# Products of zeros put among TensorE's instructions in a sparse-attention and mixture-of-experts kernel

## Chip, cores and metric

One core of a Trainium2 chip runs the whole kernel. The metric is the device time of one execution in microseconds (us), the median of several runs. The engines are named as the profile names them: PE is TensorE (PEld its weight loads), DVE is VectorE, ACT is ScalarE, POOL is GpSimd, SP issues most DMAs.

## What is computed

Two stages follow each other. The first is attention with 8 batches, 8 heads, 576 positions and 64 columns a head; half of the heads look back over 31 positions, the other half at every 32nd position. The second takes the 4608 rows of 512 columns that come out, sends each to two of eight experts and adds their weighted outputs.

```python
scores = np.where(masks, scale * q @ k.T, -1e9)          # local or strided mask by head
attn   = exp(scores - max) / (sum + 1e-9)
x      = (attn @ v).transpose(0, 2, 1, 3).reshape(4608, 512)
noisy  = x @ w_gate + log1p(exp(x @ w_noise)) * noise     # 8 experts
top2, top2_w = two largest of noisy, softmax of them
for e in range(8):                                        # w1: 512 x 1024, w2: 1024 x 512
    out[rows of e] += top2_w * (relu(x[rows of e] @ w1[e]) @ w2[e])
```

## The kernel before, in words

The program is recorded as a list of pieces. A piece has an engine, an assumed duration, what it reads and writes, and a rank; `issue_all` takes them one by one, always the one that can start earliest by the planner's own clock (`now` for each engine, `free` for each of the eight PSUM banks A to H), and emits its instructions. So the order on every engine is set by the planner's assumed durations, while the chip runs that order at its own pace. `left_a` counts PE's pieces of the attention that are still to come.

The attention goes in 32 units, one for two heads of a batch, local and strided by turns. For each unit PE transposes keys and queries (`tr` in `prep`, lines 510 and 514), adds masks and multiplies queries by keys (555, 562), transposes the exponentials `ex` that ACT writes at line 593, block by block (`tr` in `item`, 603), multiplies them by the values (622, 627) and transposes the finished block `xo` (693, 689). DVE and ACT read every bank in between: maxima (589), exponentials, copies (288, 289, 291), the scaled output `xo` (643). After each batch `route` computes the gate, the two experts of each row, and a place in the expert's list. SP brings q, k, v and writes zeros to the output; POOL scatters the list's entries.

The experts' work is cut into 32 jobs, four for each expert, of 256 or 384 rows, or of 256 with a tail of 64. The early jobs are planned between the pieces of the attention. A job has a first layer (`layer1`: for each of 8 blocks of 128 hidden columns 12 products with the rows as moving columns, line 1057) and a second layer (`layer2`: products of 512 columns, line 1107). Both split each number into a high and a low part, so three products stand for one. In the first layer of a job with a tail, branches on the expert's length (`half_used`) choose the width; in the second layer `half_block` computes the tail, or, where the tail is not used, writes one product of zeros of 512 columns (line 1116) so that the bank is defined.

At the start `issue_all` emits 20 products of zeros (line 337, `warm` is a bf16 view of a tile of zeros) into bank H. They are the only such products ahead of the change apart from line 1116.

Of the kernel before, what the change touches and what calls it, by code (L numbers as in the profile page):

```python
# [22 lines left out]
def kernel(  # L23
# [12 lines left out]
    nc = tc.nc  # L36
# [59 lines left out]
    warm = zeros.bitcast(BF16)  # L96
# [199 lines left out]
    def issue_all(expert_banks, t_start):  # L296
        now = dict(t_start)
        free = {t: 0.0 for t in BANKS}
        held, filler = [0], [False]
        marks, paced = {"ACT": [], "DVE": []}, [0.0]  # L300
        left_a = sum(1 for o in pieces if not o.expert and o.eng == "PE")
        owed = 0.0
        wire = 0.0
        for o in pieces:
            o.need = len(set(o.deps) | set(o.order))
            o.next = []
        for o in pieces:
            for x in set(o.deps) | set(o.order):
                x.next.append(o)
        for o in pieces:  # L310
            for s in o.psums:
                s.left = len(s.users)
        ready = [o for o in pieces if o.need == 0]

        def at(o, e):
            t = max(now[e], o.t0)
            for x in o.deps:
                t = max(t, x.end + (o.far if x.lat else HOP[x.e].get(e, 150)))
            for x in o.order:
                t = max(t, x.start)  # L320
            if o.lat and e == "SP":

                t = max(t, wire - (1500 if o.bulk else 5000))
            if o.psums:
                n = len(o.psums)
                if o.expert and left_a and held[0] >= expert_banks:
                    return None
                if len(free) < n or not o.expert and e == "PE" and filler[0] and (
                        len(BANKS) - len(free) - held[0] + n - 1 >= ATT_BANKS):
                    return None  # L330
                t = max(t, sorted(free.values())[n - 1] + 220)
            return t


        pw = psum.tile([128, 512], F32, name="bankH")
        for i in range(NWARM):
            nc.tensor.matmul(pw[:, :256], warm[:, :128], warm, start=True, stop=True)
        now["PE"] += 214.0 * NWARM
        done = 0
        while ready:  # L340
            best = None
            per = {}
            filler[0] = any(o.expert and o.psum for o in ready)
            for o in ready:
                for e in (("ACT", "DVE") if o.eng == "ANY" else (o.eng,)):
                    t = at(o, e)
                    if t is not None:
                        per.setdefault(e, []).append((t, o.rank, o))
            for e, c in per.items():
                m = min(x[0] for x in c)  # L350
                x = min((y for y in c if y[0] <= m + 120), key=lambda y: (y[1], y[0]))
                if e == "PE" and left_a and owed > 0:

                    x = min((y for y in c if y[2].expert and y[0] <= now["PE"] + 120), key=lambda y: (y[1], y[0]), default=x)
                if x[2].eng == "ANY":
                    other = [y for y in per.get("DVE" if e == "ACT" else "ACT", []) if y[2] is x[2]]
                    if other and other[0][0] + (40 if e == "ACT" else 0) < x[0]:
                        continue
                if best is None or x[0] < best[0]:
                    best = (x[0], e, x[2])  # L360
            t, e, o = best
            o.e, o.start = e, t
            for s in o.alloc:
                s.t = s.ring.fixed[s.ring.hist.index(s) % s.ring.k] if s.ring.fixed else s.ring.make()
            for s in o.psums:
                s.tag = min(free, key=lambda x: free[x])
                del free[s.tag]
                s.t = psum.tile([128, 512], F32, name="bank" + s.tag)
                s.x = o.expert
                held[0] += o.expert  # L370
            last = o.fn(o)
            if e in marks and getattr(last, "ins", None) is not None:
                marks[e].append((o, last))
            if e == "POOL" and o.lat:


                for engine in ("DVE", "ACT"):

                    behind = [x for x in marks[engine][-40:] if paced[0] < x[0].end <= t - 200]
                    if behind:  # L380
                        x = max(behind, key=lambda x: x[0].end)
                        for y in last if isinstance(last, list) else [last]:
                            tc.add_manual_dep(y.ins, x[1].ins.name, mybir.DependencyInfo(
                                mybir.DependencyClass.Sync, mybir.DependencyReason.DATA), reason="in its time")
                        break
                paced[0] = t
            d = o.dur if not isinstance(o.dur, dict) else o.dur[e]
            now[e] = t + d
            o.end = t + d
            if o.lat:  # L390
                wire = max(wire, t + d + 650) + o.lat * o.wires / RATE
                o.end = wire + 1500
            for s in o.touch:
                if s.ring is None:
                    s.left -= 1
                    s.last = max(getattr(s, "last", 0), o.end)
                    if s.left == 0:
                        free[s.tag] = s.last
                        if s.x:
                            held[0] -= 1  # L400
            if e == "PE" and not o.expert:
                left_a -= 1
            if e == "PE":
                owed = max(-1500.0, owed - d) if o.expert else min(3000.0, owed + PACE * d) if filler[0] else 0.0
            ready.remove(o)
            done += 1
            for x in o.next:
                x.need -= 1
                if x.need == 0:
                    ready.append(x)  # L410
        assert done == len(pieces), (done, len(pieces))
# [495 lines left out]
    def experts(zero):  # L907
# [129 lines left out]
        def half_used(e):  # L1037
            if e not in counts:
                counts[e] = nc.values_load(over[:1, E + 1 + e:E + 2 + e], engines=[mybir.EngineType.PE], min_val=0,
                                           max_val=NTOK)  # L1040
            return counts[e]

        def layer1(n, f, rank):
            e, (start, nb, tail, hb) = jobs[n]
            width = nb * 128 + tail
# [4 lines left out]
            ps = Slot()  # L1050
# [3 lines left out]
            def products(which, width):  # L1054
                for m in which:
                    d, a, c = todo[m]
                    nc.tensor.matmul(ps.t[:, :width], a.t[:, 128 * d:128 * d + 128], c.t[:, d, :width], start=(m == 0),  # L1057
                                     stop=(m == len(todo) - 1))

            def mm(o):  # L1060
                last = len(todo) - 1
                if not tail:
                    return products(range(last + 1), width)

                products([0], width)
                with tc.If(half_used(e) > tail // 2) as used:
                    products(range(1, last), width)
                with used.Else():
                    with tc.If(half_used(e) > 0) as some:
                        products(range(1, last), width - tail // 2)  # L1070
                    with some.Else():
                        products(range(1, last), width - tail)
                products([last], width)
            Piece("PE", 12 * 0.4555 * width + 30, mm, rank, read=[xh, xl, whi, wlo], psum=ps, expert=True,
                  after=lengths_known if tail else [])
            Piece("ACT", act(width) + 30, lambda o: nc.scalar.activation(hh.t[:, :width], ps.t[:, :width], AF.Relu), rank,
# [119 lines left out]
    for u in range(NU):  # L1196
# [10 lines left out]
        if u % (2 * NP) == 2 * NP - 1:  # L1207
            route(units[u][0], rank + 9, init, gates)
    experts(zero)
    issue_all(4, {"PE": 1000.0, "ACT": 2000.0, "DVE": 4500.0, "POOL": 14000.0, "SP": 600.0})  # L1210

    actx.close()
# [5 lines left out]
    with tc.If(longest > CAP):  # L1218
        with ExitStack() as octx:
# [4 lines left out]
            for e in range(E):  # L1224
                left = nc.values_load(over[:1, e:e + 1], engines=ENG, min_val=0, max_val=NTOK - CAP)
                with tc.If(left > 0):
                    nc.sync.dma_start(w1t, dram(w1, e * DM * FF, [[FF, 128], [128 * FF, ND], [1, FF]]))
                    nc.sync.dma_start(w2t, dram(w2, e * DM * FF, [[DM, 128], [128 * DM, NF], [1, DM]]))
                    with tc.For_i(0, left, 128) as it:
# [20 lines left out]
                        for f in range(NF):  # L1250
                            ph = psO.tile([128, 128], F32, name="oph", bufs=2)
                            for d in range(ND):
                                nc.tensor.matmul(ph, w1t[:, d, 128 * f:128 * f + 128], xt[:, d, :],
                                                 start=(d == 0), stop=(d == ND - 1))
# [4 lines left out]
                        o = ow.tile([128, DM], F32, name="oo")  # L1259
# [30 lines left out]
```

## Time and profile before

| what | us |
|---|---|
| median of 3 runs | 1081.55 |
| lowest, highest | 1073.44, 1081.84 |
| the profiled execution, its own time | 1080.12 |
| its span, first to last instruction | 1078.3 |
| mean granted clock of TensorE over the span | 0.981 of full speed |

The times of rows and stages are those of the one profiled execution; its span is 1.8 us shorter than its time. A busy PE in the profile is a PE with an instruction under way, not one at its peak rate.

### The profile page before, as it was taken

To read this page: it belongs to the slowest core of one execution; us is meant where nothing else is said; L and a number is where in the kernel's file an instruction comes from. 1 tells how busy PE (TensorE), PEld (TensorE's weight loads), DVE (VectorE), ACT (ScalarE), POOL (GpSimd) and SP (SyncE) were. 2 spreads that over 40 slices of the span, in tenths; PEclk is the share of its full clock that TensorE was granted. 3 is DMA by queue.
4 is the path that set the end of the run, shared out by engine and by line. 5 is a ranking of instruction groups with operands and counts; after the bars stand their busy time and mean duration, and the time that the engine had idled before them with its cause. 6 is when DMAs were issued, how large, how long until landed. Compare 5 with 4: busy or idle time off the path is not lost.

```text
span 1078.3 us, 23248 instructions
## 1 busy us (share of the span) xinstructions
PE 1049.8 (97%) x8637; PEld 936.9 (87%) x8637; DVE 559.2 (52%) x1536; ACT 477.1 (44%) x1203; POOL 543.6 (50%) x661
## 2 busy tenths in 40 slices
PE   8989999999999999999999999999999999999995
PEld 7767788988888999999998989898989898899994
DVE  6878887865863145427562455245524542363330
ACT  6878787866762234225342234223422432252220
POOL 1044354516153576647575556464636564766321
PEclk8998899999999999999999999999999999999998
DMA  8998989979871235426563245225522552352221
GB/s 178 238 227 185 216 200 259 210 209 214 245 188 42 37 65 139 111 45 171 117 173 57 51 105 144 45 51 121 130 45 56 121 128 43 63 152 53 42 36 23
DMA packets 168429, 133.01 MB, mean 123 GB/s; under 512 B 51864, under 2 KB 136344, under 8 KB 168296
## 3 DMA queue, kind: packets, MB, share of 16 engines
q1 hardware_dynamic: 145160, 92.31, 33.5%
q0 software_dynamic: 23136, 38.94, 19.7%
q8 instruction: 82, 1.34, 0.5%
q14 instruction: 51, 0.42, 0.1%
HBM read 92.85 MB, written 39.39 MB: 123 GB/s over the span
## 4 chain that ended last, share of the span: by engine, by line
PE 90%; ACT 3%; DVE 2%; issue 2%; DMA 1%; POOL 0%; SPq 0%; POOLq 0%; ACTq 0%; DVEq 0%
PE bankB L1107 6%; PE bankE L1107 5%; PE bankA L1107 5%; PE bankC L1107 5%; PE bankH L1057 5%; PE bankF L1107 5%; PE bankC L1057 5%; PE bankG L1057 5%; PE bankE L1057 5%; PE bankF L1057 5%; PE bankB L1057 5%; PE bankD L1057 5%; PE bankA L1057 5%; PE bankG L1107 4%; PE bankH L1107 3%; PE bankD L1107 3%
## 5 line engine op out<-in xcount | busy, mean ns | idle before, releaser
L980 POOL DMA_INDIRECT xg<-x_dram,gxx x248 | 257.0, 1036 | 157.0 <-DVE xr L1019 77.3
L1143 POOL DMA_INDIRECT out_dram<-res,tabt x80 | 136.1, 1701 | 100.8 <-ACT res L289 58.2
L829 POOL DMA_INDIRECT tab<-ent,addr x96 | 93.1, 970 | 61.2 <-issue 19.0
L1019 DVE STREAM_TRANSPOSE xr<-xg 128x512 f32<-128x512 f32 (+1 forms) x66 | 68.2, 1033 | 44.1 <-DMA xg<-x_dram,gxx 42.7
L1028 DVE TENSOR_TENSOR xlo<-xr,xhi 128x512 fp32r<-128x512 f32 (+1 forms) x66 | 43.6, 660 | 37.1 <-ACT xhi L1026 36.1
L1026 ACT CAST xhi<-xr 128x512 fp32r<-128x512 f32 (+1 forms) x66 | 38.9, 589 | 50.0 <-DVE xr L1019 50.0
L900 DVE TENSOR_TENSOR w1lo<-wraw,w1hi 128x512 fp32r<-128x512 f32 x80 | 54.5, 686 | 3.7 <-ACT w1hi L899 0.8
L900 DVE TENSOR_TENSOR w2lo<-wraw,w2hi 128x512 fp32r<-128x512 f32 x80 | 51.6, 683 | 0.9 <-ACT w2hi L899 0.6
L899 ACT CAST w1hi<-wraw 128x512 fp32r<-128x512 f32 x80 | 48.8, 616 | 3.2 <-DMA wraw<-in_moe_w_dram 2.9
L989 POOL TENSOR_SCALAR gix<-tabt 128x2 int32<-128x2 int32 (+1 forms) x32 | 8.1, 253 | 81.3 <-DMA tabt<-tab 79.9
L899 ACT CAST w2hi<-wraw 128x512 fp32r<-128x512 f32 x80 | 46.8, 617 | 2.1 <-DMA wraw<-in_moe_w_dram 1.3
L1057 PE MATMUL bankH<-xhi,w1hi 128*128 128x256 f32 (+3 forms) x132 | 39.9, 303 | 0.0
L1057 PE MATMUL bankC<-xhi,w1hi 128*128 128x256 f32 (+3 forms) x132 | 39.9, 302 | 0.0
L1057 PE MATMUL bankG<-xhi,w1hi 128*128 128x256 f32 (+3 forms) x132 | 39.8, 302 | 0.0
L1057 PE MATMUL bankH<-xhi,w1lo 128*128 128x256 f32 (+3 forms) x132 | 39.4, 299 | 0.0
L1057 PE MATMUL bankC<-xhi,w1lo 128*128 128x256 f32 (+3 forms) x132 | 39.4, 299 | 0.0
L1057 PE MATMUL bankC<-xlo,w1hi 128*128 128x256 f32 (+3 forms) x132 | 39.3, 298 | 0.0
L1057 PE MATMUL bankH<-xlo,w1hi 128*128 128x256 f32 (+3 forms) x132 | 39.3, 298 | 0.0
L817 POOL COPY ent<-wt 96x12 f32<-96x12 f32 x8 | 2.0, 249 | 73.8 <-DVE wt L811 73.7
L1057 PE MATMUL bankG<-xhi,w1lo 128*128 128x256 f32 (+3 forms) x132 | 39.1, 297 | 0.0
L1057 PE MATMUL bankG<-xlo,w1hi 128*128 128x256 f32 (+3 forms) x132 | 39.0, 296 | 0.0
L1107 PE MATMUL bankB<-w2hi,hhi 128*128 128x512 f32 x96 | 38.9, 405 | 0.0
(678 smaller groups left out, 3543.5 us busy)
## 6 DMA issues: line engine op xcount, KB each, us to landing
wraw<-in_moe_w_dram SPq DMA_DIRECT2D x160, 256.0 KB
out_dram<-zeros SPq DMA_DIRECT2D x12, 768.0 KB
ks<-in_k_dram SPq DMA_DIRECT2D x15, 320.0 KB
qs<-in_q_dram SPq DMA_DIRECT2D x15, 320.0 KB
vraw<-in_v_dram SPq DMA_DIRECT2D x30, 160.0 KB
raw<-in_k_dram SPq DMA_DIRECT2D x16, 288.0 KB
v_l<-in_v_dram SPq DMA_DIRECT2D x16, 288.0 KB
raw<-in_q_dram SPq DMA_DIRECT2D x16, 288.0 KB
```

Of the source, the lines that this page charges most:

```text
L817: nc.gpsimd.tensor_copy(s["ent"].t[:, :, :, 1].bitcast(F32), s["wt"].t)
L829: st = nc.gpsimd.indirect_dma_start(out=tab, out_offset=bass.IndirectOffsetOnAxis(ap=s["addr"].t[:, t, kk:kk + 1], axis=0), in_=s["ent"].t ...
L899: Piece("ACT", 620, lambda o: nc.scalar.copy(hi.t, raw.t), rank, read=[raw], alloc=[hi], expert=True)
L900: Piece("DVE", 715, lambda o: nc.vector.tensor_tensor(lo.t, raw.t, hi.t.bitcast(F32), ALU.subtract), rank, read=[raw, hi], alloc=[lo], exp ...
L980: dma(lambda o, g=g: nc.gpsimd.indirect_dma_start(out=xg.t[:, g, :], out_offset=None, in_=x_dram[:4 * known, :], in_offset=bass.IndirectOf ...
L989: nc.gpsimd.tensor_scalar(gi.t[:, :nb], tb.t[:, :nb, 0], known - 1, None, op0=ALU.min)
L1019: Piece("DVE", 8.8 * rows, lambda o, xg=xg, xr=xr, ng=ng, rows=rows: nc.vector.transpose(xr.t.rearrange("p (c x) -> p c x", c=ND)[:, :, :r ...
L1026: Piece("ACT", 620 * rows // 128, lambda o, view=view, cols=cols: nc.scalar.copy(xh.t[:, :, cols], view()), rank, read=[xr], expert=True, ...
L1028: Piece("DVE", 725 * rows // 128, lambda o, view=view, cols=cols: nc.vector.tensor_tensor(xl.t[:, :, cols], view(), xh.t[:, :, cols].bitca ...
L1057: nc.tensor.matmul(ps.t[:, :width], a.t[:, 128 * d:128 * d + 128], c.t[:, d, :width], start=(m == 0), stop=(m == len(todo) - 1))
L1107: nc.tensor.matmul(ps.t, HT[n, f][p[0]].t[:, cols], W2[n][f][p[1]].t, start=(m == 0), stop=(m == len(todo) - 1))
L1143: st = nc.gpsimd.indirect_dma_start(out=out[:known, :], out_offset=bass.IndirectOffsetOnAxis(ap=places(), axis=0), in_=y.t[:rows, :], in_o ...
```

## The change

Two kinds of products of zeros are added, each one weight load of zeros and one product of 256 columns in bf16.

The first stands in `issue_all`: as long as there are pieces of the attention to come, a PE piece with one bank that starts later by the planner's clock than PE and its bank allow is preceded by products into that same bank, one for each 150 ns of the planned gap after the first 150. The piece's own first product starts its accumulation anew. The planner's clock is not advanced for them.

The second stands in `layer1`: a job of 256 columns without a tail gets one product of zeros into its bank ahead of its first product.

```diff
             for s in o.psums:
                 s.tag = min(free, key=lambda x: free[x])
+                bank_free = free[s.tag]
                 del free[s.tag]
...
+            if e == "PE" and left_a and len(o.psums) == 1:
+                room = t - max(now["PE"], bank_free + 220)
+                for i in range(int((room - 150) // 150)):
+                    nc.tensor.matmul(o.psums[0].t[:, :256], warm[:, :128], warm, start=True, stop=True)
             last = o.fn(o)
...
             def mm(o):
                 last = len(todo) - 1
                 if not tail:
+                    if f == 0 and width == 256:
+                        nc.tensor.matmul(ps.t[:, :256], warm[:, :128], warm, start=True, stop=True)
                     return products(range(last + 1), width)
```

In the changed program 137 products of the first kind stand in 32 groups of 1 to 14, all ahead of the first product of line 1057, and 16 of the second kind. Apart from them the order of all five engines is the same. In the changed program the old lines from 369 on are 5 higher, those behind line 1062 are 7 higher.

PE's order in the attention, at about 123 us of the trace of before (`ks`, `ex` and `xo` are operands of transposes), before:

```order
L514 MATMUL bankF<-ident,qs 128x72 x4
L514 MATMUL bankC<-ident,ks 128x72 x4
L603 MATMUL bankG<-ident,ex 72x128 x4
L693 MATMUL bankH<-ident,xo_147 128x128 x4
L603 MATMUL bankE<-ident,ex 72x128 x4
```

The same place in the changed program, from the last of six pairs ahead of bank G on:

```order
L375 LDWEIGHTS zeros
L375 MATMUL bankG<-zeros 128x256
L608 MATMUL bankG<-ident,ex 72x128 x4
L375 LDWEIGHTS zeros
L375 MATMUL bankH<-zeros 128x256
L375 LDWEIGHTS zeros
L375 MATMUL bankH<-zeros 128x256
L698 MATMUL bankH<-ident,xo_147 128x128 x4
L608 MATMUL bankE<-ident,ex 72x128 x4
```

Six pairs stand now ahead of the transposes into bank G and two ahead of those into bank H; nothing else moved.

PE's order where a job of 256 columns follows the second layer of the job before it, before:

```order
L1107 MATMUL bankC<-w2hi,hhi 128x512
L1107 MATMUL bankC<-w2lo,hhi 128x512
L1107 MATMUL bankC<-w2hi,hlo 128x512
L1057 MATMUL bankA<-xhi,w1hi 128x256
L1057 MATMUL bankA<-xlo,w1hi 128x256
```

The same place in the changed program:

```order
L1114 MATMUL bankC<-w2hi,hhi 128x512
L1114 MATMUL bankC<-w2lo,hhi 128x512
L1114 MATMUL bankC<-w2hi,hlo 128x512
L1069 LDWEIGHTS zeros
L1069 MATMUL bankA<-zeros 128x256
L1062 MATMUL bankA<-xhi,w1hi 128x256
L1062 MATMUL bankA<-xlo,w1hi 128x256
```

One pair stands now between the two layers, into the bank of the job's first block.

## Rows read from the trace of the kernel before

**Rows 1.** The page: busy us, share of the span and instructions of each engine

```profile
PE 1049.8 (97%) x8637; PEld 936.9 (87%) x8637; DVE 559.2 (52%) x1536; ACT 477.1 (44%) x1203; POOL 543.6 (50%) x661
```

**Rows 2.** Busy time by stage; columns as in the first line

```profile
core 0: us, PE busy (x) PEld busy (x) DVE busy (x) ACT busy (x) POOL busy (x), PEclk, DMA share, GB/s
...
13.80:24.04 10.24, 10.24 (x116) 8.78 (x116) 6.60 (x20) 6.35 (x19) 0.00 (x0) 0.50 0.77 162
24.04:85.48 61.44, 54.12 (x1011) 44.08 (x1007) 49.77 (x214) 51.10 (x173) 13.40 (x29) 1.00 0.93 229
85.48:95.72 10.24, 9.85 (x102) 8.38 (x104) 7.96 (x23) 7.98 (x23) 6.01 (x12) 0.50 1.01 197
95.72:116.20 20.48, 18.19 (x292) 14.23 (x290) 17.59 (x80) 17.40 (x58) 6.45 (x13) 1.00 0.86 185
116.20:126.44 10.24, 10.24 (x116) 8.88 (x114) 6.75 (x27) 6.82 (x22) 4.56 (x8) 0.50 0.82 200
126.44:143.76 17.32, 16.43 (x321) 13.47 (x317) 15.10 (x50) 13.60 (x43) 11.88 (x23) 1.00 1.00 224
...
352.71:1053.99 701.28, 701.28 (x4206) 641.20 (x4204) 304.75 (x556) 225.89 (x457) 402.54 (x396) 1.00 0.40 88
```

**Rows 3.** Chain of waits by line: 116.20 to 126.44 us, then 24.04 to 85.48 us

```profile
by line: PE bankD L562 10.7%; PE bankB L622 10.4%; PE bankG L603 8.3%; PE bankH L693 8.3%; PE bankE L603 8.3%; PE bankE L510 6.6%; PE bankC L510 5.7%; PE bankF L514 4.7%; PE bankG L514 4.7%; PE bankC L514 4.7%; PE bankD L555 4.2%; PE bankB 
...
by line: ACT ex L593 8.8%; DMA raw<-in_k_dram 5.9%; issue 3.8%; PE bankE L603 3.6%; PE bankA L622 3.1%; ACT kT_s L288 2.9%; DVE mi L766 2.7%; ACT ex L595 2.7%; DVE xT L291 2.5%; DVE xo L643 2.4%; PE bankG L739 2.3%; PE bankF L603 2.2%; ACT 
```

**Rows 4.** Chain of waits in order of time: start us, us on the chain, what

```profile
1.12 4.45 PE bankH L337 x20
...
28.57 1.54 ACT ex L593 x8
...
75.86 3.63 DMA raw<-in_k_dram
103.02 6.53 DMA v_l<-in_v_dram
```

**Rows 5.** Timeline of PE: start us, us, instruction, [idle us before <- what ended it]

```profile
10.54 0.94 PE L603 MATMUL bankA<-ident,ex 128*72 128x128 f32 x4 [0.49 <-ACT ex L593]
...
28.84 0.93 PE L603 MATMUL bankH<-ident,ex 128*72 128x128 f32 x4
...
34.70 1.01 PE L603 MATMUL bankD<-ident,ex 128*96 128x128 f32 x4 [0.34 <-ACT ex L593]
...
56.99 0.63 PE L693 MATMUL bankC<-ident,xo 128*128 128x128 f32 x4 [1.53 <-ACT ex L593]
57.46 0.60 PE L603 MATMUL bankG<-ident,ex 128*72 128x128 f32 x4
57.89 0.27 PE L689 MATMUL bankH<-ident,xo 128*128 128x128 f32 x1
59.08 0.69 PE L622 MATMUL bankA<-v_s,aT 72*64 72x65 f32 x16 [0.91 <-DVE aT L291]
...
81.13 0.69 PE L622 MATMUL bankE<-v_l,aT 96*64 96x65 f32 x16
...
85.83 1.11 PE L693 MATMUL bankB<-ident,xo 128*128 128x128 f32 x4 [0.90 <-DVE xo L643]
...
97.50 1.01 PE L603 MATMUL bankD<-ident,ex 128*96 128x128 f32 x4 [0.62 <-ACT ex L593]
...
113.06 1.00 PE L603 MATMUL bankC<-ident,ex 128*96 128x128 f32 x4 [0.91 <-ACT ex L593]
```

**Rows 6.** Line 1057 in two jobs: stretch, us, PE busy, PEld busy, PEclk, DMA

```profile
843.25:854.56 11.31, 11.31 (x96) 11.26 (x95) 1.00 0.70 160
...
943.20:954.27 11.07, 11.07 (x96) 11.01 (x96) 1.00 0.65 164
```

**Rows 7.** Timeline ahead of these jobs: a weight load, a product of zeros

```profile
843.03 0.19 PEld L1057 LDWEIGHTS bankB<-xhi,w1hi 128*128 128x128 f32 x1
...
943.16 0.39 PE L1116 MATMUL bankC<-zeros 128*128 128x512 bf16 x1
```

## The prediction

> **What bounds the kernel now.** I read the page first, then the busy table by stage, then the chain of waits in the early stages, the timeline of PE there, and last the first-layer jobs one by one.
>
> The page says PE: 97% busy over the span [rows 1]. The table by stage says where that is not the whole story [rows 2]. From 352.71 us to 1053.99 us PE has no idle time at all, so there every added column of PE work is added to the end, and every column saved is taken off it. Before that lies the attention, where PE, DVE, ACT and the DMA queues are all at 75 to 100% and none is the bound alone. Whatever time the attention saves reaches the end, because the experts' PE work behind it is a fixed amount without gaps; what it loses does too.
>
> [...] Ahead of the falls PE had idled: 0.49 us at 10.54, and 0.91 us at 113.06; the 0.90 us that ended at 85.83 began ahead of the fall at 85.48 [rows 5]. But idling alone does not tell a fall: 1.53 and 0.91 us at 56.99 and 59.08 [rows 5] are the longest of all, and the clock stayed up.
>
> **The change, part by part.** It takes nothing away and moves nothing; each engine's order is what it was, with 153 weight loads and products of zeros put into PE's.
>
> *Price of one.* The 20 products of the same form at the start took 4.45 us [rows 4], 0.22 each, at a time from which no clock is recorded; 256-column products of the first layer take 11.31 / 96 = 0.118 us at full clock [rows 6]. I take 0.11 us at full clock (half of 0.22) and 0.22 at half.
>
> *137 in the attention.* Matching the order with the timeline, 58 of them (groups of 6, 6, 14, 7, 7, 8 and 10) stand just ahead of the seven instructions that have an idle time [rows 5]. 14 at 0.11 make 1.54 us against 1.53 idle, 10 make 1.10 against 0.91, 7 make 0.77 against 0.91 and 0.90, 8 make 0.88 against 0.62, 6 make 0.66 against 0.49 and 0.34. Where they are longer than the idle time, the transposes of `ex` behind them are mostly paced by ACT, which writes it block by block, and catch up. Cost about nothing.
>
> The other 79 stand where PE had no idle time in the trace: the planner's clock believed in a gap that the chip did not have. All of them on the path would be 79 x 0.11 = 8.7 us. Of these, 21 (ahead of 11.38, 28.84, 63.82, 70.00 and 113.97) stand ahead of transposes such as those at 28.84, which at full clock follow each other every (0.93 - 0.27) / 3 = 0.22 us where those at 56.99 take (0.63 - 0.3) / 3 = 0.11 [rows 5]; the 0.22 is ACT's pace (eight activations in 1.54 us on the chain at 28.57, [rows 4]), so a late start is made up. 26 stand in the three stretches at half clock (10, 8 and 8); if the clock holds, PE's work there halves and they fall into the slack. 32 are left, 3.5 us of delay on PE, the largest group of them 11 ahead of the values at 81.13 [rows 5], 1.2 us. What is late next is an evacuation by DVE or ACT, and some of the delay is found back in the next wait. I take +2.5 us; the bounds are 0 and +8.7. Each first product also takes over the wait for its bank that the real instruction had; all of PE's queue stands behind it, as it did before, and the planner puts it 220 ns after the bank's planned release, so I give that no price.
>
> *The three stretches at full clock.* Upper bound: PE is the whole path and its time halves, 3 x 10.24 / 2 = 15.4 us. Lower bound if all three go: DVE's work in them is 6.60 + 7.96 + 6.75 = 21.3 us, and in the stretch 24.04 to 85.48 DVE keeps 49.77 / 61.44 = 0.81 of the time [rows 2], so 21.3 / 0.81 = 26.3 us would do for what took 30.7: 4.4 us saved. DMA is a cover of the same kind: it is at 0.93 in the long stretch [rows 2], and the chain already waits for loads at 75.86 and 103.02 [rows 4]. The three times of the kernel lie 8.4 us apart, about what three falls more or less would make. I take -7.0, nearer to the DVE bound than to the PE bound. If no fall goes, it is 0.
>
> Whether the clock holds: the zeros of the warm-up were followed by full clock, so such products count as work, and ahead of each of the three falls stand groups of them (10 at 10.5 to 11.4, 11 at 81.1 and 7 at 85.8, 15 from 111 to 114). [...]
>
> *16 ahead of the first-layer jobs of 256 columns.* PE has no gap there, so each is paid: 0.11 us, or up to 0.19 if the next weight load (0.19 us, [rows 7]) is exposed; 16 make +1.8 to +3.0. But the 14 jobs from 352 us on come in two sorts. Eleven take 11.31 us like the one at 843.25; three take 11.07 like the one at 943.20 [rows 6]. What differs is what stands ahead: in those three the product of zeros for an unused half block, at 943.16 [rows 7]. With that product the job ends at 954.27, so the two together take 11.11 us, less than the 11.31 of the job alone: the products run at about 0.113 instead of 0.118 us, and keep that for the whole job. A lead of 256 columns instead of 512 should do the same for 11.00. Then eleven jobs save 0.31 (0.20 if it costs as much as the long one), 2.2 to 3.4; the three pay 0.11 for nothing, and so do the two jobs amid the attention: -0.55. I take -2.2. Bounds -2.9 and +3.0.
>
> **Sum**, against the profiled execution (span 1078.3, time 1080.12, within 1.5 us of the median 1081.55): 1080.1 - 7.0 + 2.5 - 2.2 = 1073.4 us.
>
> **Rivals.**
> - *The clock holds, and PE was the path.* The chain rows for it [rows 3], DVE's share and the DMA against it. -15 instead of -7: 1080.1 - 15 + 2.5 - 2.2 = 1065.4. [...]
> - *The lead does not set the pace.* For it: it has half the columns of the product seen to do so, and the jobs after wide real products have the slow pace too. +2.4 in place of -2.2: 1078.0.
> - *One or two falls stay or come elsewhere*, since the zeros shift the idle times rather than remove them: 2.3 to 4.7 us given back, 1075.7 to 1078.1.
> - *Slower: the clock falls as before.* Then the 79 lie on a path that is PE's in those stretches, 26 of them at 0.22: 53 x 0.11 + 26 x 0.22 = 11.5, of which some 8 reach the end, and the leads cost 3.0: 1080.1 + 8 + 3 = 1091. It decides if the granted clock is still 0.50 for some 30 us of the attention. For it: 56.99 and 59.08 show that idle time does not tell a fall; against it, where the groups stand.
>
> **How the numbers follow.** Forecast as summed 0.42, PE as the path 0.17, no pace from the lead 0.17, falls left 0.14, slower 0.10. About 1% (10.8 us) is what a measurement of this kernel can tell from no change: faster means under 1070.7, slower over 1092.4. The first rival is faster, and so is the part of the forecast where the stretches give 10 or more (0.12 of the 0.42); the slower rival lies just at the other bound, and I put 0.07 of it beyond. Faster 0.29, same 0.64, slower 0.07. The range 1063 to 1084 takes in the first three rivals and stops short of the slower one.
>
> **What would show it.** The table by stage: granted clock 1.00 from 24 us (or 7 us) to the tail, and the first first-layer product some 5 us ahead of 143.76. The jobs of 256 columns at 10.9 us behind their lead instead of 11.31, all alike. The transposes at the seven idle places start when they did, less what came earlier. Wrong: a stretch at 0.50 within the attention; jobs still at 11.31; idle times of DVE and ACT that now end on PE's products of zeros, or loads on the chain in the place of PE's rows.

## The result and the profile after

| | us |
|---|---|
| before, median of 16 runs | 1081.83 (1073.44 to 1086.1) |
| changed, median of 16 runs | 1070.15 (1068.19 to 1073.68) |
| ratio | 0.9896, 95% interval 0.9882 to 0.9911 |
| profiled execution of the changed kernel: time, span | 1068.83, 1067.1 |
| its granted clock over the span | 0.996 |

The changed kernel is faster by 1.04%, 11.7 us between the medians. The forecast was 1073.4 with a range of 1063 to 1084; a second measurement of the same kernel, further below, gave a ratio of 0.9923.

The page's first lines of the changed kernel, busy time and the span in 40 slices, answer to [rows 1]:

```profile
PE 1045.7 (98%) x8790; PEld 932.9 (87%) x8790; DVE 558.4 (52%) x1536; ACT 475.8 (45%) x1203; POOL 543.5 (51%) x661
...
PEclk9999999999999999999999999999999999999998
```

PE holds 153 products more and is busy 4.1 us less (1049.8 before), as it would be if work that ran at half clock now runs at full. No slice but the last has a clock under 9. The busy table by stage, cut where [rows 2] was cut and then at the first first-layer product, has the same columns as there:

```profile
13.80:24.04 10.24, 10.20 (x206) 8.50 (x205) 8.71 (x32) 8.31 (x23) 0.00 (x0) 1.00 0.98 207
24.04:85.48 61.44, 59.59 (x1030) 49.64 (x1020) 51.08 (x214) 51.80 (x177) 15.40 (x33) 1.00 1.00 227
85.48:95.72 10.24, 10.13 (x193) 8.69 (x194) 9.24 (x28) 9.40 (x32) 7.66 (x15) 1.00 1.12 220
95.72:116.20 20.48, 18.93 (x313) 15.62 (x312) 17.33 (x88) 16.89 (x54) 5.07 (x12) 1.00 0.96 223
116.20:126.44 10.24, 10.18 (x204) 8.99 (x203) 9.55 (x31) 9.16 (x31) 8.07 (x16) 1.00 1.01 228
126.44:135.10 8.66, 8.19 (x145) 6.61 (x141) 7.33 (x24) 6.99 (x23) 6.29 (x11) 1.00 1.07 239
135.10:344.06 208.96, 207.37 (x2356) 180.88 (x2355) 142.38 (x525) 138.37 (x388) 91.48 (x149) 1.00 0.80 193
344.06:1042.61 698.55, 698.55 (x4220) 636.34 (x4219) 304.13 (x556) 225.21 (x457) 401.77 (x395) 1.00 0.42 89
```

All three falls, the stretches that [rows 2] has at 0.50 (PE alone on the chain in the row for 116.20, [rows 3]), are at 1.00, and in the same 10.24 us DVE does 8.71, 9.24 and 9.55 us of work where it did 6.60, 7.96 and 6.75. The first product of the first layer starts at 135.10 us where it started at 143.76: 8.66 us gained in the attention, 8.65 of which are still there at the first job that PE does without a gap (344.06 against 352.71). PE's last instruction ends 11.38 us earlier than before, so the experts give another 2.7. DMA, at 0.92 of the time up to the first first-layer product before, is now at 1.00.

The timeline of PE at four places, the columns as in [rows 5]; line 375 is the new product in the attention, line 1069 the one ahead of a job:

```profile
52.57 1.69 PE L375 MATMUL bankC<-zeros 128*128 128x256 bf16 x14
54.17 0.66 PE L698 MATMUL bankC<-ident,xo 128*128 128x128 f32 x4
...
77.39 1.36 PE L375 MATMUL bankE<-zeros 128*128 128x256 bf16 x11
78.68 0.69 PE L627 MATMUL bankE<-v_l,aT 96*64 96x65 f32 x16
...
105.99 1.25 PE L375 MATMUL bankC<-zeros 128*128 128x256 bf16 x10
108.02 1.00 PE L608 MATMUL bankC<-ident,ex 128*96 128x128 f32 x4 [0.78 <-ACT ex L598]
...
832.49 0.28 PE L1069 MATMUL bankB<-zeros 128*128 128x256 bf16 x1
832.53 0.36 PE L1062 MATMUL bankB<-xhi,w1hi 128*128 128x256 f32 x1
832.73 0.28 PE L1062 MATMUL bankB<-xlo,w1hi 128*128 128x256 f32 x1
```

The 14 products fill what was 1.53 us of idle time and nothing is idle ahead of line 698. The ten at 105.99 leave 0.78 us idle, since ACT is still the later one there. The busy time of line 1062 (1057 before) in the jobs:

```profile
832.46:843.51 11.05, 11.05 (x98) 11.02 (x98) 8.80 (x16) 6.25 (x14) 5.95 (x7) 1.00 0.71 161
932.05:943.06 11.01, 11.01 (x98) 11.00 (x97) 8.80 (x16) 6.92 (x15) 7.09 (x6) 1.00 0.68 163
```

The first is the job that stood in [rows 6] with 11.31 us: from the start of its lead at 832.49 to its end at 843.51 it takes 11.02, so 0.29 less with the lead than without. The second was one of the three quick ones.

### The profile page after: what moved, and what is told of

It is laid out like the page before. It is cut to its first block, busy times and chain, and to the rows that moved or that the text cites. A ratio compares the mean times of both kernels' runs of the same rounds, so it can differ in the third digit from the quotient of the medians.

```text
span 1067.1 us, 23536 instructions
## 1 busy us (share of the span) xinstructions
PE 1045.7 (98%) x8790; PEld 932.9 (87%) x8790; DVE 558.4 (52%) x1536; ACT 475.8 (45%) x1203; POOL 543.5 (51%) x661
## 4 chain that ended last, share of the span: by engine, by line
PE 89%; ACT 3%; DVE 2%; issue 2%; DMA 2%; POOL 0%; POOLq 0%; DVEq 0%; ACTq 0%
PE bankB L1114 6%; PE bankE L1114 5%; PE bankA L1114 5%; PE bankC L1114 5%; PE bankF L1114 5%; PE bankC L1062 5%; PE bankG L1062 5%; PE bankE L1062 5%; PE bankH L1062 5%; PE bankF L1062 5%; PE bankA L1062 5%; PE bankD L1062 5%; PE bankB L1062 4%; PE bankG L1114 4%; PE bankH L1114 3%; PE bankD L1114 3%
## 5 line engine op out<-in xcount | busy, mean ns | idle before, releaser
L1150 POOL DMA_INDIRECT out_dram<-res,tabt x80 | 133.7, 1671 | 100.6 <-ACT res L289 51.5
```

What stands on the lines that cost most here:

```text
L1150: st = nc.gpsimd.indirect_dma_start(out=out[:known, :], out_offset=bass.IndirectOffsetOnAxis(ap=places(), axis=0), in_=y.t[:rows, :], in_o ...
```

## The experiments

The theory to be tested: the attention's 8.7 us come from the clock, which no longer falls, and the zeros there cost little; the 2.7 us of the experts come from the leads. The rivals: the zeros do cost what the forecast had, and the clock gives more; or one part does it all.

Ten runs were made, the last with the changed kernel again, each beside runs of the kernel before on the same chip. The medians of before differ by over 1 us between them (1081.75 to 1083.15), so ratios are compared.

**Each part alone.** The first kernel leaves the leads out, the second the products in the attention:

```diff
 first kernel, in layer1
-                    if f == 0 and width == 256:
-                        nc.tensor.matmul(ps.t[:, :256], warm[:, :128], warm, start=True, stop=True)
 second kernel, in issue_all
-            if e == "PE" and left_a and len(o.psums) == 1:
-                room = t - max(now["PE"], bank_free + 220)
-                for i in range(int((room - 150) // 150)):
-                    nc.tensor.matmul(o.psums[0].t[:, :256], warm[:, :128], warm, start=True, stop=True)
```

> The 137 products of zeros in the planned gaps of the attention, without the 16 ahead of the first-layer jobs. My theory (the attention gains some 8.7 us because the granted clock stays at full, and the 16 leads gain 2.7 us by the pace of eleven jobs): granted clock 1.00 through the attention, eleven jobs of 256 columns at 11.31 us again, about 1072.9 us. Rival (the leads' gain in one profile is an accident of the order of jobs and gives nothing in the time): 1070.2 us.

> The 16 leads alone, no products of zeros in the attention. My theory: stretches at granted clock 0.50 in the attention as before, all jobs of 256 columns at 10.9 us behind their lead, 1081.8 - 2.7 = 1079.1 us. Rival (leads give nothing): 1081.8 us. Second rival (the attention's gain was made in the experts, by the leads): near 1073.

Measured: the attention's part alone 1073.73 us, ratio 0.9911 (0.9876 to 0.9945); the leads alone 1080.76 us, ratio 0.9971 (0.9948 to 0.9993), before 1083.15. Both parts gain, some 9.6 and 3.1 us by the ratios, and together they make about the whole. The leads' gain agrees with 2.7 us, but with its interval of 0.8 to 5.6 us the time alone would not settle it. The jobs do: in the profile without leads eleven jobs of 256 columns take 11.31 us and three 11.08, as before, and in the profile of the leads alone all fourteen take 10.98 or 10.99 from their first real product on.

The busy table of the kernel with leads alone, cut at the stretches that its clock spent at half:

```profile
9.27:19.51 10.24, 9.51 (x99) 7.43 (x99) 5.76 (x14) 6.61 (x19) 0.00 (x0) 0.50 1.08 223
57.05:63.88 6.83, 6.26 (x72) 5.08 (x72) 3.88 (x13) 4.76 (x14) 5.14 (x10) 0.50 1.04 225
87.77:91.18 3.41, 3.36 (x18) 2.85 (x19) 3.01 (x12) 2.85 (x10) 2.60 (x5) 0.50 1.25 206
98.01:101.42 3.41, 3.41 (x25) 2.88 (x26) 2.42 (x5) 3.23 (x13) 1.68 (x3) 0.50 0.85 173
118.49:128.73 10.24, 10.24 (x117) 8.77 (x121) 6.24 (x26) 6.31 (x22) 4.32 (x7) 0.50 0.85 219
```

The order in the attention is that of before to the last instruction, and the clock falls five times instead of three, at other places: at 57 us too, where it stayed in the trace of before. So a place is no safe sign of a fall, and the three falls that the forecast looked at were three of several possible ones.

**Price of half clock.** Every run has its mean granted clock, and the stretches read from these profiles stand at 0.50 or at 1.00; so the time at half clock is put at 2 x (1 - clock) x span (41 us in the profiled execution of before, where the stretches at 0.50 add up to 40.55). Over the 40 runs of before that stood beside the first eight experiments, the time rises by 0.30 us for each us at half clock (standard error 0.05); their mean is 45 us. In the profiled execution of before 9.83 us at half clock lie in the tail behind the last product, from 1068.52 on. The slope is a correlation between executions: a delay elsewhere could both bring a fall and add time of its own, and these runs do not separate the two. The 30.7 us of the profiled execution are then worth 9.2 us, where the forecast had 7.0 between bounds of 4.4 and 15.4.

**Where the zeros stand.** Of the 32 groups the next kernels keep some, by a counter over the groups in the planner's loop:

```diff
+                zeros_now = int((room - 150) // 150)
+                if zeros_now > 0:
+                    group[0] += 1
-                for i in range(int((room - 150) // 150)):
+                for i in range(zeros_now if group[0] in KEPT else 0):
```

> Of the 137 only the 58 that stand where the trace of before shows PE idle, in seven groups, no leads. If zeros that lie on no idle time cost what my forecast had for them (2.5 us), and the clock holds with 58: 1072.9 - 2.5 = 1070.4 us. If the other 79 are free: 1072.9 with full clock. If the 79 are needed to hold the clock: one or two stretches at 0.50, 3 us each, 1076 to 1079.

> The other part of the 137: only the 79 products of zeros that stand where the trace of before shows no idle time, none in the seven idle times, no leads. If what holds the clock is that the idle times are filled: stretches at 0.50 as before and the price of 79 products on top, 1083 us or more. If it is the amount of plain products, wherever they stand: clock at 1.00 and about 1073 to 1075 us. Seen beside the run with 58 it also tells the price of a product outside the idle times: 21 more than there are 2.3 us of PE.

> Only the seven groups (43 products) that stand in the 4 us ahead of the three falls of the trace of before, no leads. If a fall is a matter of its place alone, the clock holds and the time is that of the run with 58, 1073.0 us, or a little less. If other idle times lead to falls as soon as these are gone (the clock's falls lie at other times in other executions), one or two stretches at 0.50, at 0.34 us for each us at half clock (the slope over the runs of before) 3 to 7 us more: 1076 to 1080.

Measured: the 58 in the idle times 1072.99 us, ratio 0.9905 (0.9873 to 0.9937); the other 79 alone 1078.53, ratio 0.9978 (0.9955 to 1.0002); the 43 ahead of the three falls 1075.96, ratio 0.9949 (0.9932 to 0.9965). The granted clock goes with it: the median over each kernel's runs is 0.9935, 0.9855 and 0.9895, before 0.979 and 0.978. So the 58 that fill idle time hold the clock about as well as all 137 (0.9945), the 79 hold it a little, against both sides of what was expected, and the 43 hold it less often than the 58, as expected if falls lie at other places in other executions.

**Twice as many.**

```diff
-                for i in range(int((room - 150) // 150)):
+                for i in range(2 * int((room - 150) // 150)):
```

> Twice as many products of zeros in each planned gap (274), no leads; 137 more at 0.108 us are 14.8 us more of PE. If PE's time beside the attention is free (DVE, ACT and DMA set the pace), within 2 us of the run with 137 alone, so under 1075. If a product of zeros there costs as my forecast had it (a third to a half of the exposed ones), about 1079. If PE is the path: 1087.

Measured: 1079.57 us, ratio 0.9973 (0.9951 to 0.9995), though the median clock is 0.9955, with 137 0.9945. Between 137 and 274 products lie 5.8 us for 14.8 us more of PE. The five longest pieces of this kernel's chain of waits from 24 us to the first first-layer product (start us, us, what):

```profile
55.12 3.06 PE bankC L375 x28
70.23 7.05 DMA vraw<-in_v_dram
82.30 2.40 PE bankE L375 x22
105.72 6.00 DMA ks<-in_k_dram
113.33 2.18 PE bankC L375 x20
```

Added up from 24 us to the first first-layer product, PE holds 86.8 of the 119.0 us of this chain, and 22.3 of them are products of zeros. In the changed kernel PE holds 50.3 of 111.1 us (59.4 of 119.8 before) and products of zeros 3.7; the largest single rows are others:

```profile
by line: ACT ex L598 8.0%; DMA v_l<-in_v_dram 6.4%; DMA vraw<-in_v_dram 6.2%; DVE mx L594 3.8%; issue 3.3%; PE bankA L627 2.3%; ACT ex L600 2.3%; PE bankB L627 2.3%; DVE mi L771 2.2%; ACT aT L288 2.0%; PE bankD L608 2.0%; ACT v_l L288 2.0%; 
```

**All of it on one scale.** If the clock alone made the difference, a kernel's time would be that of before less 0.30 us for each us of half clock that it lacks. The mean of before is 1083.2 us with 44.1 at half clock beside the kernels with 137, 58 and 274 products, and 1082.2 with 45.5 beside the other three. What follows from each kernel's mean time at half clock stands beside its mean measured time (kernels without leads; the transposes come below):

| kernel | us at half | by the clock alone | measured |
|---|---|---|---|
| 137 products | 12.9 | 1073.8 | 1074.0 |
| 58 in idle times | 15.5 | 1074.6 | 1073.1 |
| 79 elsewhere | 28.9 | 1077.2 | 1079.3 |
| 43 ahead of the falls | 22.8 | 1075.4 | 1076.1 |
| 137 transposes | 10.4 | 1071.6 | 1073.2 |
| 274 products | 10.4 | 1073.1 | 1080.0 |

The clock accounts for the gains of all but the last. What is left tells the price of the 79: alone they lie 2.1 us above their clock, and with them the kernel of 137 lies 1.7 us higher against its clock than the one of 58. A fit over 95 single runs (before, 137, 58, 79, and those with leads, with a level of its own for each of the three sets of runs of before) gives 0.30 us for each us at half clock (standard error 0.02), +1.9 us for the 79 (0.5), -1.0 for the 58 (0.7) and -2.3 for the leads (0.4). So the rival stated above, that the zeros do cost what the forecast had and the clock gives more, is the one that fits. The medians hide the price, since in these runs the kernels that have the 79 on top of the 58 spend some 3 us less at half clock and so get about half of it back. The 137 further products cost some 6.7 us at equal clock (6.9 above their clock against 0.2).

**Does it matter what kind of product it is?**

```diff
-                    nc.tensor.matmul(o.psums[0].t[:, :256], warm[:, :128], warm, start=True, stop=True)
+                    nc.tensor.transpose(o.psums[0].t[:, :128], zeros, ident)
```

> The 137 products of zeros turned into 137 transposes of zeros of 128 columns in fp32, which take the same 0.109 us of PE each at full clock, in the same places, no leads. If transposes do not count as work that holds the clock: stretches at 0.50 as before, 1083 us or more. If they count like other products: clock 1.00 and 1073.7 us, as with plain products.

Measured: 1073.14 us, ratio 0.9921 (0.9892 to 0.9949), median clock 0.996. In its busy table by stage one short fall is left in the attention:

```profile
0.00:100.44 100.44, 93.62 (x1564) 78.69 (x1566) 80.13 (x327) 81.48 (x264) 31.13 (x85) 1.00 0.99 217
100.44:103.85 3.41, 3.41 (x31) 3.17 (x28) 1.98 (x7) 1.35 (x5) 0.00 (x0) 0.50 0.86 191
103.85:136.83 32.98, 32.04 (x586) 27.28 (x584) 29.51 (x121) 28.24 (x89) 16.67 (x30) 1.00 0.98 227
```

fp32 transposes in the same gaps hold the clock as the bf16 products do: 0.996 and 0.9945 in the median. Whether transposes with no other products about them would hold the clock was not run.

**What of the lead sets the pace of a job.** One kernel with all 137 products and a different lead ahead of each slow job:

```diff
-                    if f == 0 and width == 256:
-                        nc.tensor.matmul(ps.t[:, :256], warm[:, :128], warm, start=True, stop=True)
+                    if f == 0 and width == 256:
+                        kind = [...][leads[0]]; leads[0] += 1
+                        if kind == "again":     # the first real product, once more
+                            nc.tensor.matmul(ps.t[:, :256], whi.t[:, :128], xh.t[:, 0, :256], start=True, stop=True)
+                        elif kind == "t128":
+                            nc.tensor.transpose(ps.t[:, :128], zeros, ident)
...
+                    if f == 0 and width == 384 and n % 8 >= 4:
+                        nc.tensor.matmul(ps.t[:, :256], warm[:, :128], warm, start=True, stop=True)
```

> All 137 in the attention; ahead of the eleven slow jobs of 256 columns not the same lead but several: none, the first real product done twice, zeros of 64, 128, 512 and twice 256 columns, a transpose of zeros; ahead of half of the jobs of 384 columns, and of a second layer in every fourth job, zeros of 256 columns. To be read from the spacing of the products in each job. My theory (a product whose weights load quickly, in bf16, lets the next weight load start early, and the job keeps that lead): 0.113 us behind every lead of zeros in bf16, 0.118 behind none, behind the real product done twice and behind the fp32 transpose. Rival (any extra product does it): 0.113 behind all. The products of 384 and 512 columns: at 0.175 and 0.227 us, if they have the slow pace, 0.004 less behind a lead; if theirs is another limit, unchanged.

It ran once, so only the spacing is read. The busy time of the real products of ten of the eleven jobs, each from its own first product to the start of what follows it:

```profile
347.84:359.15 11.31, 11.31 (x96) 11.27 (x96) 1.00 0.01 1
371.07:382.06 10.99, 10.98 (x96) 10.96 (x96) 1.00 0.38 69
454.99:465.97 10.98, 10.98 (x96) 10.95 (x96) 1.00 0.26 36
577.45:588.84 11.39, 11.39 (x96) 11.35 (x96) 1.00 0.27 39
627.35:638.66 11.31, 11.31 (x96) 11.26 (x96) 1.00 0.67 159
682.89:693.88 10.99, 10.98 (x96) 10.95 (x96) 1.00 0.24 34
733.43:744.42 10.99, 10.98 (x96) 10.95 (x96) 1.00 0.77 168
788.72:800.11 11.39, 11.39 (x96) 11.35 (x96) 1.00 0.23 33
894.02:905.10 11.08, 11.08 (x96) 11.02 (x96) 1.00 0.23 33
993.90:1004.87 10.97, 10.97 (x96) 10.94 (x96) 1.00 0.24 33
```

In order: the real product done twice, zeros of 128 columns, of 64, a transpose of zeros in fp32, the real product twice, zeros of 128, of 64, the transpose, zeros of 512, and two products of 256. All leads in bf16 give the quick pace, 64 columns as well as 512; neither fp32 form does, though each is one more product. The 11.08 behind 512 columns is the same pace with a later second product (0.31 us after the first, where 0.20 is usual behind a lead). The eleventh job, with no lead, takes 11.31. So it is not any extra product, and not the width of the lead: of the forms tried as a lead only bf16 does it. Weights and columns were both bf16 in every such lead, so which of the two counts is not shown. The timeline at a lead of 64 columns and at a transpose:

```profile
454.95 0.20 PE L1083 MATMUL bankA<-zeros 128*128 128x64 bf16 x1
454.99 0.36 PE L1063 MATMUL bankA<-xhi,w1hi 128*128 128x256 f32 x1
455.19 0.28 PE L1063 MATMUL bankA<-xlo,w1hi 128*128 128x256 f32 x1
...
577.42 0.27 PE L1076 MATMUL bankG<-ident,zeros 128*128 128x128 f32 x1
577.45 0.36 PE L1063 MATMUL bankG<-xhi,w1hi 128*128 128x256 f32 x1
577.65 0.28 PE L1063 MATMUL bankG<-xlo,w1hi 128*128 128x256 f32 x1
```

From the lead to the second real product it is 0.24 us with 64 columns, and 0.24 with the 256 of the changed kernel (832.49 to 832.73): a narrower lead saves nothing, perhaps because the real weights behind it take their time to load, 0.19 us in the trace (188 ns, the median of line 1062); that is an estimate. The delay is not what sets the pace: behind the transpose the second real product comes 0.20 us after the first too, and the job stays slow. The wide jobs do not answer to a lead: three of the jobs of 384 columns with one took 16.85 us from the first real product on and two without 16.77, all at 0.1746 us a product; the sixth, which stands behind a product of zeros for an unused half block, keeps the slower 0.1767 with a lead as without. The second layers kept their 0.227 us a product.

The weight loads of zeros of the changed kernel, in bf16, have a median of 95 ns ahead of the jobs, those of line 1062, in fp32, 188 ns. In the job whose lead stands at 832.49 the load behind the lead's starts in the same hundredth of a us, where those after it follow each other by 0.12. Why one such product leaves the 96 behind it 0.0043 us closer (0.1135 instead of 0.1178) was not shown by any run; it stays open.

**The best of the pieces, and the changed kernel again**, on one chip: the 58 products and the leads, without the 79.

> The 58 products of zeros in the seven idle times and the 16 leads, as a candidate for less than either kernel. If the gains of both parts add up: 0.9905 of before less 2.7 us, 0.988 of before, 1070 us where before is 1082.7. If the 79 others are good for holding the clock in the executions in which the falls lie elsewhere: about the same as the changed kernel or up to 2 us slower.

> The changed kernel as it was, on the same chip as the candidate, so that the two can be compared: 0.9896 of before as measured, 1071.5 us where before is 1082.7.

Measured: 1072.25 us, ratio 0.9917 (0.9888 to 0.9947), and for the changed kernel 1072.11 us, ratio 0.9923 (0.9899 to 0.9947). No difference that can be measured; no version beats the changed kernel. The 58 cost less but hold the clock a little less well: their runs spend 17.5 us at half clock in the mean, the changed kernel's 13.9, and in their profile one fall of 10.24 us is left, at 85.56. At equal clock the kernel without the 79 would be 1.5 us ahead, once more about their price. The changed kernel's second ratio overlaps with its first; the two together say 0.8 to 1.0%.

## Why the prediction was right

- *What bounds the kernel.* Right: what the attention gained reached the end whole (8.66 us at the first first-layer product, 8.65 at 344 us), and what the leads saved came on top.
- *The clock holds.* Right, and for the reason given, work put into PE's idle times; the kernel with 58 shows it (median clock 0.9935, before 0.979). But the forecast took the three falls of one execution as the place to look, and that was luck: the runs with 43 products and with the leads alone show falls at other places. It also called 1.53 and 0.91 us the longest idle times of all; one of before was longer, the clock stayed up behind it too, and no products stand ahead of it in the changed kernel:

```profile
72.68 0.63 PE L693 MATMUL bankC<-ident,xo 128*128 128x128 f32 x4 [1.75 <-DVE xo L643]
```

- *"I take -7.0, nearer to the DVE bound than to the PE bound."* Mis-sized, and the larger part of the miss: 9.2 by the slope of the runs. The DVE bound took DVE's share of 0.81 in the long stretch as what it could keep; with the clock up, DVE did 8.5 to 9.3 us of work in 10 (8.71, 9.24 and 9.55 in 10.24), so it was not the limit that the row made it seem. Over the whole attention its share went from 0.78 to 0.83 only.
- *"I take +2.5 us"* for the 79 outside the idle times. About right in size, 1.9 us (standard error 0.5), but not from the groups that the forecast had exposed, and that was luck. Of the 3.7 us of zeros on the changed kernel's chain 2.2 are products of the 79. The eleven ahead of the values at 81.13, its largest exposed group, are not among them; the five ahead of the transposes at 28.84 (0.55 us) and the eight at 123 to 125 (0.88), which it had as made up or in the slack, are.
- *The attention* was -4.5 in the sum. By the fit it is -9.2 - 1.0 + 1.9 = -8.3, and the one profile gave -8.7.
- *Leads, -2.2.* Right: eleven jobs save 0.29 (0.31 forecast), the three quick ones pay 0.12 each, and the profile shows 2.7 in all. The rival that half the columns would not do fell: an eighth does.
- *"PE was the path"*, 1065.4, was the nearest rival, 4.75 us off where the forecast was 3.25 off. Its 0.5 us for each us at half clock is more than the 0.30 measured.
- *The slower rival* fell at its own deciding point, the granted clock.
- *Signs.* One sign of being wrong came in part: loads hold 14.0 us of the chain from 24 us to the first first-layer product where they held 10.2. The jobs came as forecast, all alike, at 10.98 us behind their lead.
- *What can be told from no change.* The forecast took 1% for it, and 1070.15 lies just under its line of 1070.7, on the side to which it gave 0.29. The interval of the ratio, 0.9882 to 0.9911, tells much less than 1%.

## What to carry to other kernels

Price a throttled stretch from the spread of your own runs, time against granted clock, before pricing it from one profile: here that gave 0.30 us for each us at half clock, between the two bounds that one profile allowed. Work put into an engine costs by degrees: here nothing that the runs can tell in its idle times, 1.9 of some 8.5 us where it had none, 6.7 of 14.8 for as many products again. Before calling such work free, compare at equal clock: the medians of 58 and 137 products are alike because the price of the 79 and the clock that they gave back hid each other. Where a long run of equal products comes in two spacings, look at what stands ahead of it; a repair of 0.12 us bought 0.4 in each job.

## What was not expected of the hardware

The clock's falls wander between executions of the same order (85 and 116 us in one, 57, 88, 98 and 118 in another). 96 products of 256 columns in a row keep one of two spacings, 0.1178 (11.31 us) or 0.1135 (10.98, with 0.20 for the first), and in every such job the quicker one came behind a product in bf16 and the slower one behind fp32. In a job with a tail, products of 256 columns behind one of 320 in fp32 stood at 0.114 (482.23 to 483.37 us of before). Products of 384 columns showed 0.1746 and 0.1767, which no lead changed, those of 512 one spacing, 0.227. And transposes of zeros held the granted clock as well as products did (0.996 and 0.9945).
